# Gated MLP: values normalised on ACT instead of DVE, transposes one output tile later, last stores from two queues

## The chip, the cores and the metric

The kernel runs on one core of a Trainium2 chip. The metric is the device time of one execution in microseconds, as the median of several runs. The engines are TensorE (PE: matmuls and transposes; PEld is its weight load), VectorE (DVE), ScalarE (ACT), GpSimd (POOL) and SyncE (SP, which here only issues DMAs). Each engine works through its own instructions in order; they meet through semaphores.

## The reference

Three layers are computed on 4 batches of 576 positions: attention with a relative bias, a ReLU MLP with layer norm, and a gated MLP. The change lies in the last one. Its `x` has the shape (4, 576, 512), `d_ff` is 1024, everything is float32:

```
h = x @ w_in
h = 0.5 * h * (1 + tanh(c * (h + 0.044715 * h ** 3)))
u, v = h[..., :512], h[..., 512:]
mu = mean(v); var = mean((v - mu) ** 2)          # over the 512 columns
v_n = (v - mu) / sqrt(var + 1e-6) * g_ln
v_s = einsum('ts,bsd->btd', w_sg, v_n) + b_sg[None, :, None]
out = x + (u * v_s) @ w_out
```

## The kernel before

The engines' order is written out by hand. The gated MLP begins where the ReLU MLP's last sums come out of PSUM, at about 751 us, and runs over the four batches. Its work is a list of *groups* (`seq`, L1299 to L1303), and `step` (L1271) issues one group after the other. Every group has the form `pe_, first, second, later`: its matmuls or transposes, two rounds of work on other engines right behind them, and later stages, of which one is issued with each following step.

- `g_v(b, j)` computes one tile of 128 rows of the values: 12 matmuls of 512 columns into a PSUM tile `psa`. `first` is the square of the gelu on ACT (L1148) and a DVE instruction (L1149), `second` the tanh on ACT (L1153), DVE's L1154, which writes the tile `v` and is the last to read `psa`, and the statistics on DVE (`bn_stats` L466, `bn_aggr` L467). Then come the later stages: with the next step, `scale` (POOL: L470 adds the epsilon, L471 takes the power -1/2), `apply` (the normalisation, L482 on DVE) and `post` (`split_hi`, L110 on ACT); with the step after that `late_` (`split_lo`, L113 on POOL). Tile 4 holds the last 64 rows of two batches and is computed with batches 0 and 2, so these have five value tiles and the others four.
- `g_u(b, m)` does the same for the other half of the columns, with 24 matmuls of 288 columns and without statistics.
- `g_s(b, d)` is the gate: 28 matmuls of 288 columns, of which the last six take the high and the low part of the batch's last full value tile, then DVE (L1237, L1238), and the split into high and low part on ACT and POOL in the next step.
- `g_o(b, j)` is an output tile: 12 matmuls, one DVE add (L1260), a store from SP (L1262; tile 4 goes to two batches, L1265).
- `g_T(b, j)` transposes a tile of `x` for a later batch: four PE transposes into one of two PSUM tiles `pt` (L490), the high part on ACT (L110, `x2h`), the low part on DVE (L113, `x2l`), and after tile 3 two POOL copies (L107).

Within a step the issue order goes by rounds. After the group's own PE work come, for round 0, the earlier groups' stages and then its own `first`; for round 1 the earlier groups' stages (here `apply` of the value tile before) and then its own `second` (its tanh and what follows); for round 2 the earlier groups' `post`. `psa` has three buffers, `pt` two, `v` three (an output tile takes its result buffer from `v` as well).

`norm_parts` (L459) is shared with the layer norm of the ReLU MLP, which calls it with `act`: there the normalisation is one ACTIVATE with scale and bias from `rs` (L478), and POOL has two more operations to prepare them (L473, L474).

Of the kernel before, what the change touches and what calls it, by code (L numbers as in the profile page):

```python
# [93 lines left out]
def block_kernel(  # L94
# [6 lines left out]
    act, dve, pool, pe, sp = nc.scalar, nc.vector, nc.gpsimd, nc.tensor, nc.sync  # L101

    def new_pool(name, bufs, stack=None, **kw):
        return (stack or ctx).enter_context(tc.tile_pool(name=name, bufs=bufs, reuse_waits="tile", **kw))
# [4 lines left out]
    def split_hi(o, i, **kw):  # L109
        act.activation(o, i, AF.Copy, **kw)  # L110

    def split_lo(o, i, hi, eng=None):
        (eng or dve).tensor_tensor(out=o, in0=i, in1=hi.bitcast(F32), op=ALU.subtract)  # L113

    def product(ps, terms, start=True, stop=True):
        for j, (w, x) in enumerate(terms):
            pe.matmul(ps, lhsT=w, rhs=x, start=start and j == 0, stop=stop and j == len(terms) - 1)  # L117
# [148 lines left out]
    with ExitStack() as c:  # L266
# [21 lines left out]
        for f in (load_q, load_k):  # L288
# [9 lines left out]
            out=W.rearrange("p (g h) -> p g h", h=8), in0=w8.unsqueeze(1).to_broadcast([128, 4, 8]), in1=ind.unsqueeze(2).to_broadcast([128, 4, 8]), op=ALU.mult,  # L298
# [157 lines left out]
    def block_pair(p):  # L456
        return [p.tile([128, 4, 512], F32R, name="blk") for _ in range(2)]

    def norm_parts(sm, src, eps, dst, eng):  # L459

        s6 = sm.tile([128, 6], F32, name="s6")
        mv = sm.tile([128, 2], F32, name="mv")
        rs = sm.tile([128, 2], F32, name="rs")

        def stats():
            dve.bn_stats(out=s6, in_=src)  # L466
            dve.bn_aggr(out=mv, in_=s6)  # L467

        def scale():
            pool.tensor_scalar(out=mv[:, 1:2], in0=mv[:, 1:2], scalar1=eps, scalar2=1.0, op0=ALU.add, op1=ALU.mult)  # L470
            pool.tensor_tensor(out=rs[:, 0:1], in0=mv[:, 1:2], in1=mhalf, op=ALU.pow)  # L471
            if eng is not dve:
                pool.tensor_scalar(out=mv[:, 0:1], in0=mv[:, 0:1], scalar1=-1.0, scalar2=0.0, op0=ALU.mult, op1=ALU.add)  # L473
                pool.tensor_tensor(out=rs[:, 1:2], in0=mv[:, 0:1], in1=rs[:, 0:1], op=ALU.mult)  # L474

        def apply():
            if eng is act:
                act.activation(dst, src, AF.Identity, scale=rs[:, 0:1], bias=rs[:, 1:2])  # L478
            elif eng is pool:
                pool.tensor_scalar(out=dst, in0=src, scalar1=rs[:, 0:1], scalar2=rs[:, 1:2], op0=ALU.mult, op1=ALU.add)  # L480
            else:
                dve.tensor_scalar(out=dst, in0=src, scalar1=mv[:, 0:1], scalar2=rs[:, 0:1], op0=ALU.subtract, op1=ALU.mult)  # L482

        return stats, scale, apply
# [37 lines left out]
    def ln_T(blk, j):  # L522
        p = transpose4(xn[blk][j][0])
        th, tl = xT[blk]
        o = slice(128 * j, 128 * j + 128)
        split_hi(th[:, :, o], p)
        split_lo(tl[:, :, o], p, th[:, :, o])
# [112 lines left out]
    with ExitStack() as c:  # L640
        smp = new_pool("asm", 1, c)
        sm = smp.tile([128, 48], F32, name="sm")
# [228 lines left out]
        for u in range(-1, NU):  # L871
            for w in SEQ:
                du, name, *args = w.split()
                v, args = u + int(du), list(map(int, args))
# [54 lines left out]
    def T_groups(b):  # L929
        return [g_T(b, j) for j in ([4] if b % 2 == 0 else []) + [0, 1, 2, 3]]  # L930
# [4 lines left out]
    with ExitStack() as c:  # L935
# [125 lines left out]
        for blk in range(5):  # L1061
# [9 lines left out]
            T = [lambda j=j: ln_T(blk + 1, j) for j in range(len(tiles[blk + 1]))] if blk < 4 else []  # L1071
# [63 lines left out]
    sm = new_pool("qsm", 4)  # L1135
# [7 lines left out]
    def gelu(T, dst, cols):  # L1143


        def first():
            q = T["s"] = tp.tile([128, S], F32, name="sq")[:, :cols[0] * cols[1]].rearrange("p (a b) -> p a b", a=cols[0])
            act.activation(q, T["p"], AF.Square, scale=GELU_SQ)  # L1148
            dve.scalar_tensor_tensor(out=q, in0=q, scalar=GELU_C, in1=T["p"], op0=ALU.add, op1=ALU.mult)  # L1149

        def second():
            q = T["s"]
            act.activation(q, q, AF.Tanh)  # L1153
            dve.scalar_tensor_tensor(out=dst(), in0=q, scalar=1.0, in1=T["p"], op0=ALU.add, op1=ALU.mult)  # L1154

        return first, second

    def g_v(b, j):
        T = {}

        def pe_():
            xh, xl = x2R[b // 2] if j == 4 else [t[:, :, 128 * j:128 * j + 128] for t in x2T[b]]
            T["p"] = psA.tile([128, 2, 512], F32, name="psa")[:, :1]
            product(T["p"][:, 0], [(x[:, k], w[:, k]) for x, w in ((xh, vh), (xh, vl), (xl, vh)) for k in range(4)])
            if j == 0:
                vn[b] = block_pair(wb)
            if j == 4:
                vr[b // 2] = [vp.tile([128, 512], F32R, name="vre"), vp.tile([128, 512], F32R, name="vro")]

        def dst():  # L1170
            T["v"] = tv.tile([128, 512], F32, name="v")
            return T["v"].unsqueeze(1)

        first, second_ = gelu(T, dst, (1, 512))

        def second():
            second_()
            T["n"] = norm_parts(sm, T["v"], 4e-6, T["v"], dve)
            T["n"][0]()

        def parts():

            if j < 4:
                return [(slice(0, 128), vn[b][0][:, j], vn[b][1][:, j])]
            e, o = vr[b // 2]
            return [(slice(0, 64), e[:64], e[64:]), (slice(64, 128), o[64:], o[:64])]

        def post():
            for r, hi, _ in parts():
                split_hi(hi, T["v"][r])  # L1190

        def late_():
            for r, hi, lo in parts():
                split_lo(lo, T["v"][r], hi, pool)

        return pe_, first, second, [(lambda: T["n"][1](), lambda: T["n"][2](), post), (late_, None, None)]

    def g_u(b, m):
        T = {}

        def pe_():
            h, l = x2T[b]
            if m == 0:
                uT[b] = up.tile([128, 4, 2, 288], F32, name="u")
            ps = psA.tile([128, 2, 512], F32, name="psa")
            T["p"] = ps[:, :, :288]
            terms = [(w[:, k, 128 * m:128 * m + 128], x[:, k]) for w, x in ((uh, h), (ul, h), (uh, l)) for k in range(4)]
            for q, (w, x) in enumerate(terms):
                for z in range(2):
                    pe.matmul(ps[:, z, :288], lhsT=w, rhs=x[:, 288 * z:288 * z + 288], start=(q == 0), stop=(q == len(terms) - 1))  # L1210

        return (pe_,) + gelu(T, lambda: uT[b][:, m], (2, 288)) + ([],)
# [37 lines left out]
    def g_o(b, j):  # L1250
        T = {}

        def pe_():
            gh, gl = gr[b // 2] if j == 4 else [t[:, :, 128 * j:128 * j + 128] for t in gT[b]]
            T["p"] = psA.tile([128, 2, 512], F32, name="psa")[:, 0]
            product(T["p"], [(x[:, k], w[:, k]) for x, w in ((gh, oh), (gh, ol), (gl, oh)) for k in range(4)])

        def first():
            o = tv.tile([128, 512], F32, name="v")
            dve.tensor_tensor(out=o, in0=T["p"], in1=x_sb[:, 4 * b + j if j < 4 else 16 + b // 2], op=ALU.add)  # L1260
            if j < 4:
                sp.dma_start(out=out[b, 128 * j:128 * j + 128], in_=o)  # L1262
            else:
                for q in range(2):
                    sp.dma_start(out=out[b - 1 + q, 512:], in_=o[64 * q:64 * q + 64])  # L1265

        return pe_, first, None, []

# [16 lines left out]
    def idle():  # L1285
        return (lambda: None), None, None, []

    def v_groups(b):
        return [g_v(b, j) for j in ([4] if b % 2 == 0 else []) + [0, 1, 2, 3]]

    def mix(*lists):

        return [g for n in range(max(map(len, lists))) for x in lists for g in x[n:n + 1]]

    s = {b: [g_s(b, d) for d in range(4)] for b in range(B)}
    u = {b: [g_u(b, d) for d in range(4)] for b in range(B)}
    o = {b: [g_o(b, j) for j in range(4)] + ([g_o(b, 4)] if b % 2 else []) for b in range(B)}
    t = {b: T_groups(b) for b in range(1, B)}
    seq = v_groups(0) + u[0] + mix(s[0][:3], t[1]) + [s[0][3]] + u[1]  # L1299
    seq += [t[2][0]] + v_groups(1) + mix(o[0], t[2][1:]) + mix(s[1], u[2])  # L1300
    seq += v_groups(2) + mix(o[1], t[3]) + mix(s[2], u[3])
    seq += v_groups(3) + o[2][:2] + [idle()] + s[3] + o[2][2:] + o[3]
    seq += [idle() for _ in range(4)]  # L1303
    for n, g in enumerate(seq):
# [78 lines left out]
```

## Time and profile before

| | us |
|---|---|
| median of 3 runs | 981.34 (980.88 to 982.04) |
| the profiled execution's own time | 982.66 |
| its span, first to last instruction | 980.7 |
| PE busy in the span | 937.7 (96%) |
| PEld busy | 813.9 (83%) |
| DVE busy | 754.9 (77%) |
| ACT busy | 485.7 (50%) |
| POOL busy | 450.9 (46%) |

All times inside the trace are microseconds from the start of the span. A busy time says how long instructions of an engine were running; a line of the timeline gives the start, the duration, and in square brackets how long the engine had been idle before it and what ended the wait. Matmuls are pipelined, so their durations overlap; the distance from start to start is the time that one takes.

### The profile page before, as it was taken

Reading aid. Unit: us, or ns where it says so; the run is one execution under the profiler, and the core shown is the slowest. Engines: PE = TensorE matmul, PEld = TensorE weight load, DVE = VectorE, ACT = ScalarE, POOL = GpSimd, SP = SyncE. Lnnn points to the kernel's source line nnn. Section 1 sums busy time; section 2 is a strip of 40 time slices with the busy share of each in tenths; the row PEclk is TensorE's granted clock in tenths of the full one; section 3 lists DMA queues with packets and bytes.
Section 4 is the critical chain, followed back from the end, with each engine's and each line's share of the span. In section 5 each row is a group of like instructions: output and inputs, shape, how many; then the busy total and the mean of one; then the engine's idle time right before and its main releaser. Section 6 shows DMA issues by size and latency. Waiting matters only on the chain. (4 is left out here: it accounts for less than half of the span.)

```text
span 980.7 us, 16000 instructions
## 1 busy us (share of the span) xinstructions
PE 937.7 (96%) x5729; PEld 813.9 (83%) x5729; DVE 754.9 (77%) x1460; ACT 485.7 (50%) x1090; POOL 450.9 (46%) x556
## 2 busy tenths in 40 slices
PE   7879999999898999999999999999999999998998
PEld 2269998989898878888888888888888897988986
DVE  8989888899887858886769797979765847475462
ACT  8969987989797854322222222323132434242320
POOL 0086997989899744332314334333300423132241
PEclk9999999999999999999999999999999999999999
DMA  7875445436443271113022333332213000001002
GB/s 245 280 265 187 160 153 181 152 124 199 140 143 121 67 257 68 44 31 106 21 99 93 119 95 119 95 118 91 101 65 121 1 2 22 22 1 54 1 23 75
DMA packets 53007, 104.49 MB, mean 107 GB/s; under 512 B 9152, under 2 KB 20160, under 8 KB 52672
## 3 DMA queue, kind: packets, MB, share of 16 engines
q1 hardware_dynamic: 52096, 103.02, 31.3%
q8 instruction: 45, 0.74, 0.3%
q10 hardware_dynamic: 832, 0.46, 0.2%
q14 instruction: 34, 0.28, 0.1%
HBM read 75.08 MB, written 28.38 MB: 105 GB/s over the span
## 5 line engine op out<-in xcount | busy, mean ns | idle before, releaser
L170 POOL TENSOR_TENSOR cvl<-cvl,cvt 128x512 f32<-128x512 f32 x44 | 56.9, 1292 | 206.3 <-DVE cvt L167 186.8
L117 PE MATMUL psh<-blk,w1h 128*128 128x512 f32 (+1 forms) x640 | 151.4, 368 | 0.0
L636 ACT ACTIVATE hh<-psh 128x512 fp32r<-128x512 f32 (+1 forms) x80 | 43.9, 552 | 185.7 <-PE psh L117 177.7
L117 PEld LDWEIGHTS psh<-blk,w1h 128*128 128x128 f32 x640 | 113.5, 188 | 20.7 <-DVE hl L637 0.3
L689 DVE CUSTOM_DVE_ANT_0 ct<-s,bias 128x576 f32<-128x576 f32 x144 | 107.4, 753 | 24.6 <-PE s L683 15.0
L703 ACT ACTIVATE a<-ct,sm 128x576 f32<-128x576 f32 x144 | 112.2, 779 | 3.3 <-POOL v L107 2.3
L1031 DVE TENSOR_TENSOR x_sb<-psy,x_sb 128x512 f32<-128x512 f32 x144 | 97.3, 683 | 9.1 <-PE psy L117 8.6
L709 PE MATMUL pt<-ident,a 128*128 128x128 f32 x576 | 87.1, 279 | 13.8 <-DVE at0l L113 13.8
L637 DVE SCALAR_TENSOR_TENSOR hl<-psh,hh 128x512 fp32r<-128x512 f32 (+1 forms) x80 | 50.5, 633 | 56.0 <-ACT hh L636 55.9
L117 PE MATMUL psy<-w2h,hh 128*128 128x512 f32 x288 | 90.4, 395 | 0.1
L117 PE MATMUL psy<-w2l,hh 128*128 128x512 f32 x288 | 89.0, 390 | 0.0
L117 PE MATMUL psy<-w2h,hl 128*128 128x512 f32 x288 | 88.8, 390 | 0.0
L709 PEld LDWEIGHTS pt<-ident,a 128*128 128x128 f32 x576 | 70.6, 143 | 15.7 <-DVE at0l L113 15.4
L117 PE MATMUL psh<-blk,w1l 128*128 128x512 f32 (+1 forms) x320 | 79.0, 368 | 0.0
L683 PE MATMUL s<-kh,q 128*128 128x288 f32 x320 | 73.5, 320 | 2.7 <-DVE sm L689 0.9
L683 PE MATMUL s<-kl,q 128*128 128x288 f32 x320 | 66.5, 298 | 0.0
L117 PEld LDWEIGHTS psh<-blk,w1l 128*128 128x128 f32 x320 | 56.8, 189 | 10.0
L117 PEld LDWEIGHTS psy<-w2h,hl 128*128 128x128 f32 x288 | 54.1, 188 | 11.5
L117 PEld LDWEIGHTS psy<-w2l,hh 128*128 128x128 f32 x288 | 54.0, 188 | 11.4
L171 POOL TENSOR_TENSOR cvw<-cvl,cvw 128x512 f32<-128x512 f32 x44 | 59.9, 1362 | 3.5
L117 PEld LDWEIGHTS psy<-w2h,hh 128*128 128x128 f32 x288 | 52.4, 188 | 10.5 <-DVE x_sb L1031 0.8
L683 PEld LDWEIGHTS s<-kh,q 128*128 128x128 f32 x320 | 50.0, 194 | 6.0 <-POOL q L113 1.5
(193 smaller groups left out, 2233.1 us busy)
## 6 DMA issues: line engine op xcount, KB each, us to landing
r<-in_moe_w_ch_dram SPq DMA_DIRECT2D x32, 512.0 KB, 4.6
k<-in_k_dram SPq DMA_DIRECT2D x16, 640.0 KB, 5.2
q<-in_q_dram SPq DMA_DIRECT2D x16, 576.0 KB, 4.1
scr<-o SPq DMA_DIRECT2D x24, 295.5 KB, 3.7
v<-in_v_dram SPq DMA_DIRECT2D x16, 320.0 KB, 3.8
bias<-scr SPq DMA_DIRECT2D x8, 576.0 KB, 7.6
bias<-scr SPq DMA_DIRECT2D x8, 512.0 KB, 7.5
wc<-cvw SPq DMA_DIRECT2D x16, 256.0 KB, 2.4
```

What stands on the lines that cost most here:

```text
L117: pe.matmul(ps, lhsT=w, rhs=x, start=start and j == 0, stop=stop and j == len(terms) - 1)
L170: pool.tensor_tensor(out=T["l"], in0=T["l"], in1=T["t"].bitcast(F32), op=ALU.mult)
L171: pool.tensor_tensor(out=T["w"], in0=T["l"], in1=T["w"], op=ALU.add)
L636: act.activation(hh[:, f, :n], ps[:, :n], AF.Relu)
L637: dve.scalar_tensor_tensor(out=hl[:, f, :n], in0=ps[:, :n], scalar=0.0, in1=hh[:, f, :n].bitcast(F32), op0=ALU.max, op1=ALU.subtract)
L683: pe.matmul(s[:, x, :288], lhsT=w, rhs=m[:, 288 * x:288 * x + 288], start=j == 0, stop=j == len(prs) - 1)
L689: dve.tensor_tensor_reduce(out=ct, in0=s[:, :, :288], in1=bias[UNITS[u][0]][:, n].rearrange("p (a b) -> p a b", a=2), scale=-0.125, scalar ...
L703: act.activation(weights(n), ct.rearrange("p a b -> p (a b)"), AF.Exp, scale=-1.0, bias=mt, accum_out=SU[u % 2][:, n:n + 1])
L709: pe.transpose(PA[k % 2][:, j], e[:, 128 * j:128 * j + 128], ident)
L1031: dve.tensor_tensor(out=x_sb[:, t], in0=ps, in1=x_sb[:, t], op=ALU.add)
```

## The change

The change has three parts. `g_v` calls `norm_parts` with `act`, so that the normalisation of a value tile becomes one ACTIVATE (L478), with POOL's L473 and L474 ahead of it, in the place in the order where DVE's L482 stood. Behind the values of batches 1 and 2 stand the output tiles of the batch before (`o[0]`, `o[1]`) and the transposes for the batch after (`t[2]`, `t[3]`). They now alternate from the second output tile on instead of from the first: behind the values of batch 1 the order o0 T0 o1 T1 o2 T2 o3 T3 becomes o0 o1 T0 o2 T1 o3 T2 T3, behind those of batch 2 o0 T0 o1 T1 o2 T2 o3 T3 o4 becomes o0 o1 T0 o2 T1 o3 T2 o4 T3. And of the two stores of an output tile 4 the second is issued by ACT instead of SP.

```diff
         def second():
             second_()
-            T["n"] = norm_parts(sm, T["v"], 4e-6, T["v"], dve)
+            T["n"] = norm_parts(sm, T["v"], 4e-6, T["v"], act)
             T["n"][0]()
...
             else:
-                for q in range(2):
-                    sp.dma_start(out=out[b - 1 + q, 512:], in_=o[64 * q:64 * q + 64])
+                for q, e in enumerate((sp, act)):
+                    e.dma_start(out=out[b - 1 + q, 512:], in_=o[64 * q:64 * q + 64])
...
-    seq += [t[2][0]] + v_groups(1) + mix(o[0], t[2][1:]) + mix(s[1], u[2])
-    seq += v_groups(2) + mix(o[1], t[3]) + mix(s[2], u[3])
+    seq += [t[2][0]] + v_groups(1) + o[0][:1] + mix(o[0][1:], t[2][1:]) + mix(s[1], u[2])
+    seq += v_groups(2) + o[1][:1] + mix(o[1][1:], t[3]) + mix(s[2], u[3])
```

## Rows read from the trace of the kernel before

**Rows 1.** Windows, four blocks: length, busy time (instructions) by engine; sum and means
```profile
sum 109.90, PE 102.32 PEld 85.43 DVE 80.49 ACT 45.06 POOL 42.35; mean PE 25.58 PEld 21.36 DVE 20.12 ACT 11.27 POOL 10.59
```

**Rows 2.** Timeline of PE: start, duration, instruction, in brackets the idle time before
```profile
771.93 2.35 PE L1210 MATMUL psa<-x2h,blk 128*128 128x288 f32 x16 [0.58 <-DVE v L1154]
...
776.00 2.36 PE L1210 MATMUL psa<-x2h,blk 128*128 128x288 f32 x16 [0.66 <-DVE u L1154]
...
779.26 0.42 PE L1228 MATMUL psa<-sgh,vre 128*128 128x288 f32 x2
...
831.23 0.66 PE L490 MATMUL pt<-ident,x_sb 128*128 128x128 f32 x4 [1.89 <-DVE x2l L113]
831.64 3.02 PE L117 MATMUL psa<-blk 128*128 128x512 f32 x12
...
834.86 0.51 PE L1228 MATMUL psa<-sgh,vro 128*128 128x288 f32 x2
...
895.36 0.42 PE L1228 MATMUL psa<-sgh,vre 128*128 128x288 f32 x2
...
945.27 0.54 PE L1228 MATMUL psa<-sgh,blk 128*128 128x288 f32 x2 [0.55 <-POOL blk L113]
```

**Rows 3.** Timeline of DVE, one value step of batch 1
```profile
818.67 0.18 DVE L467 BATCH_NORM_AGGREGATE mv<-s 128x2 f32<-128x6 f32 x1
...
819.80 1.51 DVE L482 TENSOR_SCALAR v<-v,mv,rs 128x512 f32<-128x512 f32 x1 [0.38 <-POOL rs L471]
821.23 0.68 DVE L1154 SCALAR_TENSOR_TENSOR v<-sq,psa 128x512 f32<-128x512 f32 x1
...
822.67 0.18 DVE L467 BATCH_NORM_AGGREGATE mv<-s 128x2 f32<-128x6 f32 x1
```

**Rows 4.** Timeline of POOL, the same step
```profile
819.73 1.29 POOL L113 TENSOR_TENSOR blk<-v,blk 128x512 fp32r<-128x512 f32 x1
```

**Rows 5.** Line L482: duration min/median/max in ns, first and last start
```profile
L482 DVE TENSOR_SCALAR v<-v,mv,rs x18: 545/1508/1531, 758.5 to 941.7; 128x512 f32<-128x512 f32 x18
```

**Rows 6.** Timeline of all engines, one layer-norm step of the ReLU MLP
```profile
358.94 0.18 DVE L467 BATCH_NORM_AGGREGATE mv<-s 128x2 f32<-128x6 f32 x1
...
360.51 0.82 ACT L478 ACTIVATE t<-x_sb,rs 128x512 f32<-128x512 f32 x1 [1.17 <-POOL rs L474]
```

**Rows 7.** The same view, a later layer-norm step
```profile
386.38 0.18 DVE L467 BATCH_NORM_AGGREGATE mv<-s 128x2 f32<-128x6 f32 x1
...
388.43 0.82 ACT L478 ACTIVATE t<-x_sb,rs 128x512 f32<-128x512 f32 x1 [2.25 <-POOL rs L474]
...
389.15 0.58 ACT L636 ACTIVATE hh<-psh 128x512 fp32r<-128x512 f32 x1
```

**Rows 8.** The same view, the tanh of a value tile and what follows it
```profile
813.51 0.63 ACT L1153 ACTIVATE sq<-sq 128x512 f32<-128x512 f32 x1 [0.76 <-DVE sq L1149]
...
814.18 0.69 DVE L1154 SCALAR_TENSOR_TENSOR v<-sq,psa 128x512 f32<-128x512 f32 x1 [0.70 <-ACT sq L1153]
```

**Rows 9.** Timeline of DVE: first `bn_aggr` of batches 0 to 3, one L1154
```profile
757.34 0.18 DVE L467 BATCH_NORM_AGGREGATE mv<-s 128x2 f32<-128x6 f32 x1
...
771.11 0.68 DVE L1154 SCALAR_TENSOR_TENSOR v<-sq,psa 128x512 f32<-128x512 f32 x1
...
815.63 0.18 DVE L467 BATCH_NORM_AGGREGATE mv<-s 128x2 f32<-128x6 f32 x1
...
869.13 0.18 DVE L467 BATCH_NORM_AGGREGATE mv<-s 128x2 f32<-128x6 f32 x1
...
929.55 0.18 DVE L467 BATCH_NORM_AGGREGATE mv<-s 128x2 f32<-128x6 f32 x1
```

**Rows 10.** Timeline at the end, SP's queue
```profile
976.80 1.11 SPq L1265 DMA_DIRECT2D out_dram<-v  x2
```

**Rows 11.** DMA issues: queue, count, KB each, median us from issue to landing
```profile
out_dram<-v SPq DMA_DIRECT2D x4, 128.0 KB, 2.3
...
xs<-xr ACTq DMA_DIRECT2D x2, 16.0 KB, 5.9
```

## The prediction

> **What bounds the kernel now.** The page gives TensorE (PE) 96% of the span, so I went straight to the stretches where PE is not fed. The change touches only the gated MLP, from 750.9 us on. The table of windows for its four blocks "values and what follows them" shows PE busy for 102.3 of 109.9 us [rows 1]: 7.6 us idle, at a granted clock of 1.00. Between these blocks PE has no gap. PE's timeline then names what it waits for [rows 2]: a bank of `psa` that VectorE (DVE) still reads, `x2l` for the transposes, and at the end of batch 3 the values' low part from POOL.
>
> DVE's timeline tells why [rows 3]. A value step (one `g_v`) takes 4.00 us, from one `bn_aggr` to the next, where PE needs 2.8 (3.22 for 12 such matmuls and a transpose [rows 2]). It is a ring: the statistics of one tile, POOL's variance and power on them, L482's normalisation, then L1154, which finishes the next tile, and its statistics. DVE is not simply full: L482 starts 1.13 us after `bn_aggr`, having waited 0.38 for POOL. It takes 1.51 us where it runs beside POOL's split of an earlier tile [rows 4]; the shortest of the 18 takes 0.55, the median is 1.51 [rows 5].
>
> **The change, part by part.** *Normalisation on ACT.* It removes 18 L482 from DVE. It adds 18 ACTIVATEs with scale and bias pointers, and 36 small POOL operations (L473, L474). DVE's relief counts only if the ring gets shorter, so I put the new ring together from rows. The nearest are those of the layer norm in the first MLP, which uses this very form.
> - `bn_aggr` to the start of the normalisation on ACT, over four POOL operations: 358.94 to 360.51, 1.57 us [rows 6]. It was 1.13.
> - In a step the program issues the normalisation of tile n ahead of the tanh of tile n+1, and ACT runs in order. From its start to the next ACTIVATE's start: 388.43 to 389.15, 0.72 us [rows 7]. The tanh's input has long been ready, so the tanh now stands inside the ring; before, it ran beside it.
> - The tanh's start to L1154's start: 0.67 [rows 8]. L1154's start to `bn_aggr`: 1.44 [rows 3].
>
> Sum 1.57 + 0.72 + 0.67 + 1.44 = 4.40 us a step, against 4.00 (and 3.04 for the first step of a block, when POOL has no split to do: 815.63 to 818.67 [rows 3, 9]). What queues behind the waiting normalisation on ACT is that tanh, and DVE's L1154 and the bank of `psa` wait for it. The square of the gelu is issued ahead of it and doesn't suffer. POOL holds the four operations and one split of 1.29, under 3 us of the 4.40, so that stays hidden.
>
> *What that does to each block*, counted from the block's first `bn_aggr` [rows 9], which the change doesn't move. A bank returns 0.14 us after L1154's end: 771.11 + 0.68, and PE goes on at 771.93 [rows 2, 9]. So PE gets a tile's bank 0.62 before that tile's `bn_aggr` (1.44 - 0.68 - 0.14).
> - *Batch 0* (five tiles, then `u`): the last `bn_aggr` comes at 757.34 + 4 x 4.40 = 774.94, so the third `u` group starts at 774.32 (was 771.93). The fourth waits for the first `u` group's L1154, which stands behind the last normalisation (774.94 + 1.57 = 776.51), a tanh (777.22), 0.73 for it and 0.74 for itself (rows 8 with a tenth more for 576 columns), and 0.15: 778.84, was 776.00 [rows 2]. **+2.84**.
> - *Batch 1* (four tiles, then output tiles and transposes): the third output tile needs the last value's bank: 815.63 + 3 x 4.40 - 0.62 = 828.21. From there, two output tiles with a transpose (3.22 each) and one transpose more (0.41, 831.23 to 831.64) give 835.06 for the first gate group, was 834.86 [rows 2]. **+0.20**.
> - *Batch 2* (five tiles): 869.13 + 17.60 - 0.62 = 886.11, then three output tiles with a transpose, 9.66: 895.77, was 895.36. **+0.41**.
> - *Batch 3*: last `bn_aggr` at 929.55 + 13.20 = 942.75; +1.57 to the normalisation, +0.82 for it, +0.63 for the high part on ACT, +1.29 for POOL's low part and 0.12 of hand-overs: the last low-part matmul starts at 947.18, was 945.27 [rows 2]. **+1.91**.
>
> Sum of the four: **+5.4 us**. Past each block PE is fed without gaps, so nothing gives this back.
>
> *Transposes one output tile later.* The four PE transposes, ACT's high part, DVE's low part and, for the last one, two POOL copies all move behind one more output tile with its DVE add and its store on SP. The store waits for the add alone and holds nobody up. Before, the third transpose waits 1.89 us for the first one's `x2l` [rows 2], since that is queued behind the last normalisation; batch 2 has its like. In the sums above this wait is gone: by the same steps batch 1's first `x2l` lands near 833.1, and its user comes at 834.3. The gain, about 4 us in the two blocks, is what holds batches 1 and 2 near zero; the bank waits of the longer ring use it up. In batch 1 the last two transposes now stand together. The work on them is hidden by the gate group that follows (28 matmuls; 24 take 3.26 us, 776.00 to 779.26); without that it would cost about 1 us.
>
> *Stores from two queues.* SP needs 1.11 us to issue the last two stores [rows 10], so the second starts some 0.55 after the first. ACT would issue it at once, and the two transfers then share the DMA engines. Gain between 0 and 0.55 us; I take 0.3. For a loss: the nearest stores of ACT's queue land in 5.9 us where SP's halves take 2.3 [rows 11], +3.6 if the queue were the reason. They stand in a stretch of heavy traffic, and I take nothing for it. The same edit in batch 2 puts a store that waits for DVE's add into ACT's queue, ahead of the last transpose's high part, which comes about 1 us later. The gate group covers that too; uncovered it costs that 1 us.
>
> **Sum**: 5.4 - 0.3 = +5.1 us on the profiled execution (span 980.7, its own time 982.66). The median of the runs, 981.34, lies 1.3 below that one and takes the same shift: **986.4 us**. The total moves by 14 us for each microsecond of ring (4 + 3 + 4 + 3 steps), so 0.1 in the ring is 1.4 us, and the ring at which nothing changes is 4.40 - 5.1/14 = 4.04.
>
> **Rivals.**
> *A, faster: DVE's load is the bound, not the ring.* DVE is idle for 0.38 of 4.00 us; without L482's 1.51 it has 2.1 us of work against PE's 2.8. If the normalisation on ACT closed no ring, the 7.6 us of gaps would go: 981.3 - 7.6 - 0.3 = 973.4. For it: L482's usual form costs 0.96 above its short one. Against: the normalisation needs POOL's result on the tile before, and the tanh is ordered behind it. It decides from a ring below 4.04. The Trainium skill (SBUF — State Buffer, Who interferes with whom) says that DVE and GpSimd share one port pair under an exclusive lock, which a two-port DVE form such as `tensor_scalar` takes, while ACT never waits for anyone; by that rule alone a step would fall to 3.04. The 1.51 beside 0.55 agrees with such a lock, but it is one term of the ring only. 6%.
>
> *B, no change: the ring stays near 4.0*, because ACT's start or the added POOL operations cost less here than in the layer norm. Then 986.4 - 14 x 0.4 = 980.8. For it: the layer norm's rows stand beside other DVE work. Against: the POOL operations both have last the same. 9%.
>
> *C, slower still: POOL's long forms.* In one layer-norm step `bn_aggr` to the normalisation took 2.05 us (386.38 to 388.43 [rows 7]), beside DVE's conversions. A ring of 4.88 gives 986.4 + 14 x 0.48 = 993.1. No conversion runs in this stage. 5%.
>
> **How the numbers follow.** Forecast 80%: rings of 4.2 to 4.5 give 983.6 to 987.8, and ACT's slower queue would add up to 3.6, of which I cut the upper, unlikely half. Range 983.2 to 989.5; A, B and C fall outside with 20%. A measurement of this kernel can tell about 0.2%, 2 us, from no change. Slower by more: the forecast but its lowest edge, and C, 85%. Within: most of B and that edge, 8%. Faster: A and the part of B with a still shorter ring, 7%.
>
> **What would show it.** In the changed kernel's DVE timeline `bn_aggr` to `bn_aggr` should read 4.4 in a block, with L1154 waiting for ACT's tanh and ACT waiting for POOL's L474. PE's gaps should name L1154 three times in a row per block, at 1.0 to 1.3 us each, and no transpose should wait for `x2l`. The first gate group of batch 0 should start near 782.1 (was 779.26). A ring of 4.0 or less, or PE gaps that stay at the transposes, would prove the forecast wrong.

## The result, and the profile after

The changed kernel takes 990.75 us (median of 14 runs, 987.0 to 995.23), the kernel before, run beside it, 985.82 (14 runs, 980.88 to 989.11). The ratio is 1.0066, 95% interval 1.0047 to 1.0084; a second comparison, further down, gave 1.0049 (1.0029 to 1.0069). The forecast was a shift of +5.1 us, a ratio of 986.4 / 981.34 = 1.0052: slower, by about as much. But the time itself, 990.75, lies above the forecast's range, since the kernel before ran at 985.82 here and not at the 981.34 of the three runs shown.

The profiled execution spans 993.0 us, 12.3 more than the one of before. Its first `bn_aggr` of the gated MLP stands at 764.01, 6.67 later than before (757.34 [rows 9]), and up to there the two programs are the same. From that instruction to the end of the span there are 229.0 us, where there were 223.4: **+5.6 us** for the part that the change touches.

The table of windows over the four blocks, from the first matmul of the values to the first gate group (the last one to the end of that group), here with its sum row; it answers to [rows 1]:

```profile
sum 115.30, PE 102.39 PEld 84.63 DVE 58.43 ACT 55.77 POOL 48.58; mean PE 25.60 PEld 21.16 DVE 14.61 ACT 13.94 POOL 12.14
```

PE has the same work (102.39 against 102.32) and 12.9 us of gaps instead of 7.6. DVE has lost 22 us of work, and it didn't help. DVE's timeline of one value step of batch 1, beside [rows 3]:

```profile
825.33 0.18 DVE L467 BATCH_NORM_AGGREGATE mv<-s 128x2 f32<-128x6 f32 x1
...
828.28 0.69 DVE L1154 SCALAR_TENSOR_TENSOR v<-sq,psa 128x512 f32<-128x512 f32 x1 [2.19 <-ACT sq L1153]
...
829.73 0.18 DVE L467 BATCH_NORM_AGGREGATE mv<-s 128x2 f32<-128x6 f32 x1
```

The step is 4.40 us, and DVE stands idle for 2.19 of it, waiting for ACT's tanh. POOL's and ACT's timelines of the same step show what the tanh waits for:

```profile
825.60 0.19 POOL L470 TENSOR_SCALAR mv<-mv 128x1 f32<-128x1 f32 x1 [15.79 <-DVE mv L467]
...
826.68 0.19 POOL L474 TENSOR_TENSOR rs<-mv,rs 128x1 f32<-128x1 f32 x1
```
```profile
826.91 0.82 ACT L478 ACTIVATE v<-v,rs 128x512 f32<-128x512 f32 x1 [1.73 <-POOL rs L474]
827.63 0.61 ACT L1153 ACTIVATE sq<-sq 128x512 f32<-128x512 f32 x1
```

From `bn_aggr` to the normalisation on ACT are 1.58 us, to the tanh 0.72 more, to L1154 0.65, to the next `bn_aggr` 1.45. PE's timeline at the gaps of the four blocks, and the first gate group of each, beside [rows 2]:

```profile
772.18 2.35 PE L1210 MATMUL psa<-x2h,blk 128*128 128x288 f32 x16 [0.86 <-DVE v L1154]
...
785.70 2.36 PE L1210 MATMUL psa<-x2h,blk 128*128 128x288 f32 x16 [1.10 <-DVE u L1154]
...
788.97 0.42 PE L1228 MATMUL psa<-sgh,vre 128*128 128x288 f32 x2
...
833.51 3.00 PE L117 MATMUL psa<-blk 128*128 128x512 f32 x12 [0.87 <-DVE v L1154]
...
837.97 2.98 PE L117 MATMUL psa<-blk 128*128 128x512 f32 x12 [1.02 <-DVE v L1154]
840.79 0.60 PE L490 MATMUL pt<-ident,x_sb 128*128 128x128 f32 x4
...
844.82 0.51 PE L1228 MATMUL psa<-sgh,vro 128*128 128x288 f32 x2
...
891.81 3.01 PE L117 MATMUL psa<-blk 128*128 128x512 f32 x12 [1.53 <-DVE v L1154]
...
905.87 0.51 PE L1228 MATMUL psa<-sgh,vre 128*128 128x288 f32 x2
...
952.80 0.50 PE L1228 MATMUL psa<-sgh,vro 128*128 128x288 f32 x2 [1.48 <-DVE v L1154]
...
957.89 0.53 PE L1228 MATMUL psa<-sgh,blk 128*128 128x288 f32 x2 [0.56 <-POOL blk L113]
```

The gaps now name L1154: four in a row in batch 0, two in batch 1, three in batch 2 and two in batch 3 (not all are shown), of 0.86 to 1.53 us each; besides, PE waits for POOL's low part in batch 3. None names a transpose's `x2l` any more. At the end, SP and ACT issue the two last stores side by side; it was 1.11 us on SP alone [rows 10]:

```profile
988.70 0.69 DVE L1260 TENSOR_TENSOR v<-psa,x_sb 128x512 f32<-128x512 f32 x1 [2.03 <-PE psa L117]
989.42 0.49 SPq L1265 DMA_DIRECT2D out_dram<-v  x1
989.42 0.50 ACTq L1265 DMA_DIRECT2D out_dram<-v  x1
```

### The profile page after: what moved, and what is told of

It is laid out like the page before. It is cut to its first block, busy times and chain, and to the rows that moved or that the text cites. A ratio compares the mean times of both kernels' runs of the same rounds, so it can differ in the third digit from the quotient of the medians.

```text
span 993.0 us, 16029 instructions
## 1 busy us (share of the span) xinstructions
PE 942.0 (95%) x5729; PEld 815.2 (82%) x5729; DVE 734.0 (74%) x1442; ACT 497.0 (50%) x1108; POOL 457.6 (46%) x592
```

## The experiments

The theory is the ring: in a value step the normalisation, ahead of the next tanh on ACT, closes a loop of 4.4 us through DVE, POOL and ACT, and PE waits for the banks that this loop returns. The rivals: the moved transposes carry the loss, the ACT form itself is too dear, DVE's load is the bound, and the change delays the earlier stages. Since the programs are the same up to the first `bn_aggr` of the gated MLP, each profile is read by two numbers, the first `bn_aggr` and the time from it to the end of the span.

| kernel | first `bn_aggr` | from there to the end | against 223.4 | ratio to before (95%) |
|---|---|---|---|---|
| before | 757.34 | 223.4 | | |
| changed | 764.01 | 229.0 | +5.6 | 1.0066 (1.0047 to 1.0084) |
| same | 758.19 | 223.4 | 0.0 | 0.9998 (0.9975 to 1.0021) |
| after_again | 756.68 | 228.8 | +5.5 | 1.0049 (1.0029 to 1.0069) |
| norm_only | 758.16 | 235.8 | +12.4 | 1.0103 (1.0065 to 1.0141) |
| turn_only | 758.00 | 219.7 | -3.7 | 0.996 (0.9935 to 0.9985) |
| store_only | 761.27 | 223.0 | -0.4 | one run |
| ring_plus | 760.97 | 233.5 | +10.1 | one run |
| norm_late | 758.99 | 214.2 | -9.2 | 0.9902 (0.9872 to 0.9931) |
| dve_late | 760.51 | 229.1 | +5.7 | 1.0056 (1.003 to 1.0083) |
| dve_mid | 759.43 | 219.6 | -3.8 | 0.9962 (0.9933 to 0.999) |

### The same programs again: `same` and `after_again`

No edit; the kernel before, and the changed kernel.

> The kernel before, unchanged, as a second measurement of it. In the profiles at hand the first bn_aggr of the gated MLP stands at 757.34 us before and at 764.01 after, though the program is the same up to there; from it to the end of the span are 223.4 us before and 229.0 after. Theory (the gated MLP alone changed; the first 757 us differ from execution to execution): the ratio is 1.000, the first bn_aggr lies anywhere between 756 and 765, and from there to the end are 223.4 +- 0.3. Rival (the change itself delays the earlier stages): the first bn_aggr is at 757.3 +- 0.7 here, and all executions of this kernel agree within 0.3%.

> The changed kernel once more. Theory (the first 757 us differ from execution to execution, the gated MLP does not): from the first bn_aggr to the end again 229.0 +- 0.5 us, while the first bn_aggr lies anywhere between 756 and 765; ratio to the kernel before 1.0055. Rival (the change delays the earlier stages as well): first bn_aggr at 764 +- 1 again, ratio 1.010 or more.

The 12 runs of `same` lie between 980.94 and 991.29 us (median 985.82), the 24 runs of the kernel before beside them between 980.94 and 991.5 (985.4). From the first `bn_aggr` to the end, though, the profiles agree within 0.2 us: 223.4 and 223.4 before, 229.0 and 228.8 after. DVE's timeline of the changed kernel's second profile has the first `bn_aggr` even ahead of the one of before:

```profile
756.68 0.18 DVE L467 BATCH_NORM_AGGREGATE mv<-s 128x2 f32<-128x6 f32 x1
```

So the 6.7 us in front of the gated MLP don't belong to the change. They are the spread of the earlier stages, of which the forecast knew three runs. Most of it arises early: the first `bn_aggr` of the whole program, in the ReLU MLP's layer norm, starts at 308.8 us before and at 314.3 after, so 5.5 of the 6.7 us are there already.

### The parts alone: `norm_only`, `turn_only`, `store_only`

```diff
-            T["n"] = norm_parts(sm, T["v"], 4e-6, T["v"], dve)
+            T["n"] = norm_parts(sm, T["v"], 4e-6, T["v"], act)
```

> Only the normalisation moves to ACT; the transposes and the stores stay as before. Ring theory: bn_aggr to bn_aggr 4.4 us; the third transposes of batches 1 and 2 still wait for the first x2l, which now comes behind a later normalisation. Shifts of the blocks +3.0 (batch 0), +1.9 (1), +2.2 (2), +2.0 (3), so 223.4 + 9.1 = 232.5 us from the first bn_aggr to the end, ratio 1.009. Rival (the loss comes from the moved transposes, not from ACT): under 225, ratio near 1.000.

It is the normalisation that costs, +12.4 us, 3.3 more than expected. `bn_aggr` to `bn_aggr` is 4.4 to 4.5 as foreseen, and PE's timeline has the foreseen wait at batch 1's third transposes; but then the next output tile takes too long:

```profile
832.07 2.98 PE L117 MATMUL psa<-blk 128*128 128x512 f32 x12 [1.00 <-DVE v L1154]
...
837.00 0.66 PE L490 MATMUL pt<-ident,x_sb 128*128 128x128 f32 x4 [1.95 <-DVE x2l L113]
...
841.78 0.65 PE L490 MATMUL pt<-ident,x_sb 128*128 128x128 f32 x4
```

From the third transposes to the fourth are 4.78 us; before, they were 3.27, from 831.23 [rows 2] to

```profile
834.50 0.60 PE L490 MATMUL pt<-ident,x_sb 128*128 128x128 f32 x4
```

The windows of `norm_only` tell why; the fields are length, busy time (instructions) of PE, PEld, DVE, ACT and POOL, then the granted clock, the DMA share and GB/s:

```profile
838.40:841.90 3.50, 3.50 (x10) 2.60 (x9) 0.93 (x2) 0.00 (x0) 0.00 (x0) 0.51 0.40 149
899.90:903.30 3.40, 3.40 (x9) 2.57 (x9) 0.98 (x2) 0.00 (x0) 0.00 (x0) 0.50 0.41 154
```

In these two stretches the granted clock was at half, 1.2 GHz instead of 2.4, after the waits of batches 1 and 2. At 1.5 us each by the first, they make up 3.0 of the 3.3 us. What made the clock fall here and not in the other kernels was not tested.

```diff
-    seq += [t[2][0]] + v_groups(1) + mix(o[0], t[2][1:]) + mix(s[1], u[2])
-    seq += v_groups(2) + mix(o[1], t[3]) + mix(s[2], u[3])
+    seq += [t[2][0]] + v_groups(1) + o[0][:1] + mix(o[0][1:], t[2][1:]) + mix(s[1], u[2])
+    seq += v_groups(2) + o[1][:1] + mix(o[1][1:], t[3]) + mix(s[2], u[3])
```

> Only the transposes move behind one more output tile; the normalisation stays on DVE. Ring theory: bn_aggr to bn_aggr stays 4.0 us and 3.0 in a block's first step; the waits at the third transposes (1.9 and 2.2 us) go, batch 0 and batch 3 stay. -1.9 in batch 1 and -2.0 in batch 2: 219.5 us from the first bn_aggr to the end, ratio 0.996. Rival (the move costs): above 223.4, ratio over 1.000.

-3.7 us. In PE's timeline of batch 1 no transpose waits, and the first gate group starts 17.50 us after the batch's first `bn_aggr` (816.28); it was 834.86 - 815.63 = 19.23:

```profile
829.90 2.99 PE L117 MATMUL psa<-blk 128*128 128x512 f32 x12
832.73 1.29 PE L490 MATMUL pt<-ident,x_sb 128*128 128x128 f32 x8
833.78 0.51 PE L1228 MATMUL psa<-sgh,vro 128*128 128x288 f32 x2
```

The third part's edit is the one of the stores in the diff above.

> Only the second of two stores goes to ACT's queue. Prediction: the end comes 0.3 us sooner after the last add (976.08 to 980.72 is 4.64 before), and the store in batch 2 costs nothing: 223.1 us from the first bn_aggr to the end. Rival (ACT's queue is the slower one): its store lands 3.6 us later, 226 or more.

-0.4 us over the whole stretch, and 4.29 us from the last add (979.97) to the end of the span, where it was 4.64 (976.08 to 980.72). ACT's queue is not slower here: in the changed kernel the four half stores land in 2.4 to 2.7 us, on either queue. Without the two stretches at half clock the three parts add up to the whole: 12.4 - 3.0 - 3.7 - 0.4 = 5.3 us, against 5.6 measured.

### One more operation in the ring: `ring_plus`

```diff
             pool.tensor_tensor(out=rs[:, 0:1], in0=mv[:, 1:2], in1=mhalf, op=ALU.pow)
+            if eps == 4e-6:
+                pool.tensor_scalar(out=rs[:, 0:1], in0=rs[:, 0:1], scalar1=1.0, scalar2=0.0, op0=ALU.mult, op1=ALU.add)
```

> The changed kernel with one more small POOL operation in the chain between the power and the normalisation of the values (a multiplication of rs by 1). The nearest rows put such an operation at 0.27 us from start to start. Ring theory: bn_aggr to bn_aggr 4.4 + 0.27 = 4.67 us, and over the 14 steps of the four blocks +3.8 us: 229.0 + 3.8 = 232.8 us from the first bn_aggr to the end (a fall of the granted clock, as the kernel with the normalisation alone showed, would add some 1.7 each). Rival (the ring is not what PE waits for; POOL has room, being busy for 46% of the span): 229.0 +- 0.4.

DVE's timeline of the step in batch 1 (the edit moves L1154 to L1156 and the tanh to L1155):

```profile
823.59 0.18 DVE L467 BATCH_NORM_AGGREGATE mv<-s 128x2 f32<-128x6 f32 x1
...
826.80 0.69 DVE L1156 SCALAR_TENSOR_TENSOR v<-sq,psa 128x512 f32<-128x512 f32 x1 [2.45 <-ACT sq L1155]
...
828.25 0.18 DVE L467 BATCH_NORM_AGGREGATE mv<-s 128x2 f32<-128x6 f32 x1
```

The step grows by 0.26 us to 4.66, and the whole by 4.5 us, of which 14 x 0.26 = 3.6 are the ring's. One stretch at half clock (892.2 to 895.6 us, granted 0.51) may hold the rest; this is a single execution. So one more operation of 0.19 us, on an engine that is busy for less than half of the time, lengthens 14 steps by 0.26 us each.

### The order: `norm_late`

```diff
-        return pe_, first, second, [(lambda: T["n"][1](), lambda: T["n"][2](), post), (late_, None, None)]
+        return pe_, first, second, [(lambda: T["n"][1](), None, lambda: (T["n"][2](), post())), (late_, None, None)]
```

This is the changed kernel with the normalisation one place later on ACT, behind the next tanh.

> The changed kernel with one difference in the order: the normalisation on ACT is issued behind the next tile's tanh (together with the split after it) instead of ahead of it. Same instructions, same engines. Ring theory (it is the order that closes the ring): L1154 waits no longer for the normalisation, bn_aggr to bn_aggr falls to 2.7 to 3.2 us, all waits of PE for banks and transposes go: -2.0, -2.0, -3.3 and -2.2 us in the four blocks and -0.3 at the end, so 213.6 us from the first bn_aggr to the end, ratio to the kernel before 0.990. Rival (the ACT form itself, 0.82 us and two more POOL operations, is what costs): bn_aggr to bn_aggr stays above 4, 223 us or more, ratio 1.000 or more.

-9.2 us, and 14.8 us better than the changed kernel with the same instructions on the same engines. The timeline of DVE and ACT in batch 1:

```profile
815.51 0.18 DVE L467 BATCH_NORM_AGGREGATE mv<-s 128x2 f32<-128x6 f32 x1
...
816.30 0.63 ACT L1153 ACTIVATE sq<-sq 128x512 f32<-128x512 f32 x1 [0.94 <-DVE sq L1149]
...
816.97 0.69 DVE L1154 SCALAR_TENSOR_TENSOR v<-sq,psa 128x512 f32<-128x512 f32 x1 [0.70 <-ACT sq L1153]
817.09 0.82 ACT L478 ACTIVATE v<-v,rs 128x512 f32<-128x512 f32 x1 [0.16 <-POOL rs L474]
...
818.41 0.18 DVE L467 BATCH_NORM_AGGREGATE mv<-s 128x2 f32<-128x6 f32 x1
```

The tanh goes ahead, and L1154 starts before the normalisation has begun. The first step of a block is 2.9 us, the others 3.2 to 3.5 (4.3 once in the blocks with five tiles). Of PE's waits for banks and transposes none is left; one of 0.55 us for POOL's low part remains in batch 3. With a ratio of 0.9902 it is faster than both kernels.

### The order on DVE: `dve_late` and `dve_mid`

If the order is what counts, the same move should help with the normalisation on DVE. `dve_late` has the edit of `norm_late`, with `dve` kept in `norm_parts`.

> Transposes and stores as in the changed kernel, the normalisation on DVE as before, but issued behind the next tile's statistics instead of ahead of its L1154. Ring theory (the order, not the engine, closes the ring): bn_aggr to bn_aggr is DVE's own work, 2.8 to 3.7 us (with L482 at 0.55 or 1.51), and most of PE's waits go: 214 to 219 us from the first bn_aggr to the end, ratio 0.991 to 0.996. Rival (DVE's load is the bound, rival A of the prediction): bn_aggr to bn_aggr stays at 4.0 and the result that of the moved transposes alone, 219.5 or more.

The expectation failed: 229.1 us, and steps of 4.6 to 4.7 after a first one of 2.9 (5.4 once in the blocks with five tiles). DVE's and ACT's timelines of batch 1:

```profile
825.90 0.18 DVE L467 BATCH_NORM_AGGREGATE mv<-s 128x2 f32<-128x6 f32 x1
826.00 0.52 DVE L482 TENSOR_SCALAR v<-v,mv,rs 128x512 f32<-128x512 f32 x1
827.70 0.69 DVE L1149 SCALAR_TENSOR_TENSOR sq<-sq,psa 128x512 f32<-128x512 f32 x1 [1.18 <-ACT sq L1148]
...
830.54 0.18 DVE L467 BATCH_NORM_AGGREGATE mv<-s 128x2 f32<-128x6 f32 x1
```
```profile
826.55 0.63 ACT L110 ACTIVATE blk<-v 128x512 fp32r<-128x512 f32 x1 [2.13 <-DVE v L482]
827.09 0.58 ACT L1148 ACTIVATE sq<-psa 128x512 f32<-128x512 f32 x1
```

Another ring has closed. L482, now at the end of DVE's step, feeds the split on ACT, the next tile's square is queued behind that split, and everything in DVE's next step waits for the square. It is not DVE's load either: DVE waits 1.18 us for the square alone.

`dve_mid` puts L482 between the next L1154 and its statistics. A list `held` takes it up, and `second` empties it. The diff is against the changed kernel with `dve` put back into `norm_parts`.

```diff
             second_()
+            flush()
             T["n"] = norm_parts(sm, T["v"], 4e-6, T["v"], dve)
...
-        return pe_, first, second, [(lambda: T["n"][1](), lambda: T["n"][2](), post), (late_, None, None)]
+        return pe_, first, second, [(lambda: T["n"][1](), lambda: held.append(T["n"][2]), lambda: (flush(), post())), (late_, None, None)]
```

> The normalisation stays on DVE and is issued between the next tile's L1154 and its statistics (in the kernel before: ahead of L1154; in dve_late: behind the statistics, where ACT's high part and with it the next square came too late and the step grew to 4.6 to 4.7 us). Transposes and stores as in the changed kernel. Theory (it is the place in the order that makes the ring, on either engine): L1154 gives its bank back before the normalisation; DVE's own work is left, 3.3 to 3.7 us a step, and PE's waits get shorter in all four blocks: 215 to 219 us from the first bn_aggr to the end, ratio 0.991 to 0.996. Rival (the normalisation has to leave DVE for a gain beyond that of the moved transposes): 219.2 (219.5 for the transposes, less 0.3 for the stores) or more.

Steps of 3.7 to 3.8 us after a first one of 3.2 (4.7 once in the blocks with five tiles), but 219.6 in all: no gain over the moved transposes alone. DVE's timeline:

```profile
820.57 0.54 DVE L482 TENSOR_SCALAR v<-v,mv,rs 128x512 f32<-128x512 f32 x1
...
823.68 0.69 DVE L1154 SCALAR_TENSOR_TENSOR v<-sq,psa 128x512 f32<-128x512 f32 x1 [0.70 <-ACT sq L1153]
824.29 0.54 DVE L482 TENSOR_SCALAR v<-v,mv,rs 128x512 f32<-128x512 f32 x1
```

The loop is the same one, 3.72 us from L482 to L482 over ACT's split, the next square and its tanh. On DVE every place tried leaves one such loop per step. In `norm_late` the split still stands ahead of a square, and ACT's timeline of the later steps reads:

```profile
819.81 0.63 ACT L1153 ACTIVATE sq<-sq 128x512 f32<-128x512 f32 x1 [0.75 <-DVE sq L1149]
820.35 0.80 ACT L478 ACTIVATE v<-v,rs 128x512 f32<-128x512 f32 x1
821.19 0.63 ACT L110 ACTIVATE blk<-v 128x512 fp32r<-128x512 f32 x1
821.72 0.58 ACT L1148 ACTIVATE sq<-psa 128x512 f32<-128x512 f32 x1
823.06 0.63 ACT L1153 ACTIVATE sq<-sq 128x512 f32<-128x512 f32 x1 [0.75 <-DVE sq L1149]
```

The normalisation and the split follow the tanh without a wait for another engine, and the only wait of the round is the one for L1149: tanh, normalisation, split, square, L1149 and the next tanh take 3.25 us. So the expectation that the place alone decides was wrong as well. Of the places tried, only the late one on ACT shortened the round so far: it takes the place and the engine together.

## Why the prediction was right in its steps and wrong in its time

**The base, the step that failed.** "The median of the runs, 981.34, [...] takes the same shift." Three runs, 980.88 to 982.04, were taken as the kernel's level, and the range had no term for it. In the 79 further runs of that program single runs go from 977.96 to 991.5, with a median of 985.25, and 66 of them lie above 982.04. Nor is the level the same in every comparison: 985.82 (14 runs, the three among them) beside the changed kernel, 985.4 and 985.82 (24 and 12) with `same`, 983.65 (19) beside `after_again` and 983.65 (13) beside `dve_mid`. On 985.82 the forecast's +5.1 gives 990.9; measured were 990.75. On 983.65 it gives 988.75; `after_again` has 989.07, inside the range. On which side of the range's upper end the time fell was thus decided by the base. Where the spread sits is shown: the first `bn_aggr` lies between 756.68 and 764.01 in eleven profiles, while what follows repeats within 0.2 us for either program. What makes it is settled only in part. Of the 68 runs with a mean granted clock of their own the 13 at 0.994 or more span 976.0 to 981.1 us, the 20 at 0.989 or less 981.6 to 989.5; but at 0.993 they go from 979.0 to 985.8, so the clock is not all of it. No run was made to tell the rest apart.

**The ring: right.** Predicted 4.40 us a step as 1.57 + 0.72 + 0.67 + 1.44; measured 4.40 as 1.58 + 0.72 + 0.65 + 1.45, and 4.46 to 4.54 for the last steps of a block, which the forecast didn't have. The rows of the layer norm held for the values as they stand.

**The blocks: right, each a little short.** Between the shift of each block's first `bn_aggr` and that of its first gate group (in batch 3 the last low part), the trace has +3.04 (predicted 2.84), +0.26 (0.20), +0.54 (0.41) and +2.02 (1.91): 5.9 instead of 5.4. The small excess in all four fits the longer last steps.

**The end: right.** 4.31 us from the last add to the end instead of 4.64, -0.3 as taken; the store in ACT's queue in batch 2 cost nothing that shows.

**The transposes: right, the count of PE's waits not.** "PE's gaps should name L1154 three times in a row per block, at 1.0 to 1.3 us each"; they name it four, two, three and two times, at 0.86 to 1.53 us. The wait for `x2l` is gone, its 3.7 us (about 4 predicted) were gained by `turn_only` and, in the changed kernel, spent on the bank waits.

**The rivals.** A (DVE's load) falls: DVE lost 22 us of work, waits 1.91 to 2.33 us for the tanh in each step, and PE waits longer than before. The Trainium skill (SBUF — State Buffer, Who interferes with whom) has an exclusive lock between DVE and GpSimd and has ACT wait for nobody. The rows agree: the normalisation on ACT lasts 0.81 to 0.82 us in all 18 cases, 14 of them beside POOL's split, where DVE's L482 usually took 1.51. But this was one term of a loop that became longer elsewhere. B and C fall with the measured 4.40. The prediction left out one thing that `norm_only` and `ring_plus` then had: right after PE's longer waits the granted clock was at half for a stretch. In the two profiles of the changed kernel no such stretch lies in the gated MLP.

## What to carry to other kernels

Where engines hand tiles round in order, ask of every moved instruction which instruction of the next tile is queued behind it, and add up the loop that this closes; taking work off a busy engine gains nothing if the loop gets longer, and the same work one place later in the queue was worth 14.8 us here. Put such a loop together from the rows of the nearest place that already uses the form. And state a forecast as a shift or a ratio to a base measured beside it: three runs that agreed within 0.12% stood 4 us below the median of the 79 that followed.

## What the runs showed of the hardware that was not expected

- PE's granted clock fell to 1.2 GHz for stretches of 3.4 us within the gated MLP: from 838.4 and from 899.9 us in `norm_only`, and from 892.2 in `ring_plus`. Before them PE had waited for 0.41, 1.00 and 1.95 us in that block, for 0.86, 1.08, 1.05 and 1.93, and for 1.39 and 1.84. The kernel before waited for 1.89 us at the place of the first and for 0.59 and 2.19 at that of the second, the changed kernel in batch 2 for 0.86, 1.53 and 1.02, all without a fall. The two stretches of `norm_only` cost about 1.5 us each. What decides between the cases is not shown.
- POOL and DVE hinder each other in either order. In the kernel before L482 takes 1.51 us beside POOL's split [rows 3, 4]. In `dve_late` L482 starts first, at 826.00, and takes 0.52, and it is POOL's L470, started at 826.17, that takes 0.39 us instead of 0.19.
- A store from ACT's queue cost ACT 0.50 us at the end and landed as fast as SP's (2.4 to 2.7 us), so ACT's queue alone doesn't explain the 5.9 us of [rows 11].
